# First channel layer in units of 512 columns, narrower mask products and new list priorities in a fused block-sparse attention and mixer kernel

## The chip, the cores and the metric

The kernel runs on one core of one Trainium2 chip. The metric is the device time in microseconds; of several runs the median counts. TensorE (PE in the profile) does the matrix products, VectorE (DVE) and ScalarE (ACT) the element-wise work, GpSimd (POOL) some of the mask and most of the load issues, SyncE (SP) the other transfers.

## The reference

Block-sparse attention for 4 batches of 8 heads, 768 positions, 64 columns per head, and then a token and channel mixer on its output, reshaped to 4 x 768 x 512.

```python
scores = scale * np.matmul(q, k.transpose(0, 1, 3, 2))
mask = np.abs(blk_i - blk_j) <= window              # blocks of 32, window 1
mask = mask | (blk_i == 0) | (blk_j == 0) | (blk_i == n_blocks - 1) | (blk_j == n_blocks - 1)
for qb in range(n_blocks):
    for kb in sampled_blocks[qb]:
        mask[qb * block:(qb + 1) * block, kb * block:(kb + 1) * block] = True
scores = np.where(mask, scores, -1000000000.0)
...                                                  # softmax over the keys
x = attn @ v
h = np.maximum(xt @ w_tok1, 0.0) @ w_tok2            # token layers, 768 -> 256 -> 768
u = x + h.transpose(0, 2, 1)
h2 = np.maximum(u @ w_ch1, 0.0) @ w_ch2              # channel layers, 512 -> 1536 -> 512
out = u + h2
```

## The kernel before

Heads are worked in 16 pairs p, four pairs to a batch. Position s of the sequence sits on partition s // 6, in chunk s % 6, so that each of six chunks holds 128 positions that lie six apart. For each pair, k and q are transposed (on TensorE for pairs 1 to 7, L711, with copies by VectorE or ScalarE; by transposing transfers on SP's queue from pair 8 on, L671). The queries of a pair go in three parts t of 256, the keys in three parts jj of 256. A group of four score matmuls (L770, two key chunks by two heads) fills two of the eight PSUM banks; ScalarE takes the exponential of it in one instruction (L783) and frees the banks. The value products (L895, 24 matmuls of 65 columns per (p, t), the last column a sum) go to one bank, and VectorE normalises them (L909, L910) into the tile x of the batch.

For pairs 0 to 4 the mask is part of the scores: 24 more rows of k and q (88 rows in all) add a large negative number. From pair 5 on (`NT0`), the scores of the two heads are matmuls of 64 rows each, the three groups of a (p, t) are issued together as a unit of twelve, and the mask is multiplied into the exponentials `et` by VectorE, 3072 elements per partition in one instruction (L800).

When the four pairs of a batch are through, the two token layers follow (L976 and L998; for batch 0 in narrower pieces per pair, L1030 and L1052), with a relu between them and an addition (L1006, L1061), then the turn of u to uT (by transposing transfers, L955, for batch 0 by TensorE, L1074), and the channel layers in `ch(b)`: the first (L1110) takes 12 x 2 units of four matmuls of 384 columns, each unit with a relu by ScalarE (L939) or VectorE (L941) into `rc`; the second (L1138) takes 12 matmuls of 512 columns for each of six chunks, and VectorE adds u (L1150) and SP sends the rows out.

The order on every engine is set while the program is built, by the class `Planner`. It keeps a clock, one free time per engine and a list of operations with priorities; at each step it gives a free engine the ready operation of the lowest priority number, with costs in ns that are written beside each operation. TensorE's work comes in streams with priorities of their own: scores 0, value products 1, token layers `toks` (batch 0: `tokp`), transposes `trp`, channel layers 4. Operations of VectorE and ScalarE have the priorities `relu`, `norm`, `add`, `cut` (mask products), `fin` (last additions), `relayk` and `relayv` (copies of k, q and v), `ev2` and `ev4` (copies of transposed k and q). `later`, `unseen` and the `h_` values decide whether a bank of the scores may be lent to another product; `grace` says by how much a relu on ScalarE may delay an exponential; `m2` delays the readiness of a transpose.

Of the kernel before, what the change touches and what calls it, by code (L numbers as in the profile page):

```python
# [8 lines left out]
FP32 = mybir.dt.float32  # L9
# [4 lines left out]
KN = dict(  # L14
    tokp=2.5, trp=2.6, toks=1.2, later=1400.0, unseen=1500.0, h_pm=1200.0, h_po=1800.0,
    h_ch1=1400.0, h_ch2=3500.0, relayk=0.8, relayv=4.6, fin=2.1, relu=0.85, cut=5.0, norm=0.6,
    add=3.0, ev2=2.0, ev4=3.3, grace=400.0, m1=0.0, m2=150.0, nt0=5, cuts=2, xbar=8,
)
# [37 lines left out]
class Planner:  # L56
# [13 lines left out]
    def __init__(self, slots):  # L70
        self.now = 0.0
        self.free_at = {"pe": 0.0, "act": 0.0, "dve": 0.0, "sp": 0.0}
        self.streams = []
        self.ops = []
        self.count = 0
        self.slots = {tag: [Ev(0.0)] * n for tag, n in slots.items()}
        self.banks = [Ev(0.0)] * 8
        self.shared = 0
        self.lend = None
        self.exp_pending = 0  # L80
# [73 lines left out]
    def step(self):  # L154
# [29 lines left out]
        else:  # L184
            nxt.append(self.free_at["pe"])
        for eng in ("act", "dve", "sp"):
            if self.free_at[eng] > self.now:
# [42 lines left out]
def kernel(  # L230
# [12 lines left out]
    nc = tc.nc  # L243
# [9 lines left out]
    NET = 3  # L253
    NPE = KN["xbar"]
    NT0 = KN["nt0"]
    TOKP = KN["tokp"]
# [380 lines left out]
    def relayout(p):  # L637
        lays = {}
        for nm in ("k", "q", "v") if p >= NT0 else ("v",):
            raw = raws.pop((nm, p))  # L640
# [38 lines left out]
    def transposes(p):  # L679
        yield lambda: ("v", p) in raws  # L680
        if p >= NPE:
# [77 lines left out]
    et_rel = {u: Ev() for u in units}  # L759
    VISIT = 3  # L760
    CUTS = (((0,), (1,), (2,)), ((0, 1), (2,)), ((0, 1, 2),), ((0,), (1, 2)))[KN["cuts"]]

    def scores(s, bank, done, rel, exps):
# [30 lines left out]
        for group in CUTS:  # L794
            if group[-1] != jj:
                continue

            def cut(eng, lo=group[0], n=len(group)):
                et = ets[p, t][:, lo : lo + n, :, :, :].rearrange("k j i h q -> k (j i) h q")
                nc.vector.tensor_tensor(  # L800
                    out=et, in0=et,
                    in1=free(mask[:, 2 * lo, 256 * t : 256 * t + 256], 0,
                             [[S, 2 * n], [0, 2], [1, 256]]),
                    op=ALU.mult,
                )

            ev = P.op(("dve",), {"dve": 158.0 + 537.0 * len(group)},
                      [exps[x] for x in group] + [mask_there], cut, prio=KN["cut"])
            for x in group:
                alias(et_there[p, t, x], ev)  # L810

    def qk_deps(p, t, jj):
# [24 lines left out]
    def qk_stream():  # L837
        exps = {}
        while queue:
# [5 lines left out]
            if p < NT0:  # L845
# [13 lines left out]
                continue  # L859

            evs = [(Ev(), Ev()) for _ in range(3)]

# [12 lines left out]
            if t == 2:  # L875
                alias(qk_done[p], evs[2][0])

# [55 lines left out]

    def relu_op(o, i, deps, prio):
        n = i.free_size()

        def emit(eng):
            if eng == "act":
                nc.scalar.activation(out=o(), in_=i, func=AF.Relu)  # L939
            else:  # L940
                nc.vector.tensor_scalar(  # L941
                    out=o(), in0=i, scalar1=0.0, scalar2=None, op0=ALU.max
                )

        return P.op(("dve", "act"), {"dve": dve_psum(n), "act": act_cost(n)}, deps, emit, prio=prio)
# [19 lines left out]
    def tok(b, g):  # L965
# [21 lines left out]
        a_t = sbw.tile([128, 2, 256], BF16, tag="a_t", name=f"a_t{b}_{g}")  # L987
        a_there = relu_op(lambda: a_t[:, :, :], box["pm"][:, :, :], [last], urgent)
        alias(rel, a_there)
# [29 lines left out]
    def tok_first(p):  # L1019
# [21 lines left out]
        a_t = sbw.tile([128, 2, 256], BF16, tag="a_t", name=f"a_t0_{p}")  # L1041
        a_there = relu_op(lambda: a_t[:, :, 0:128], box["pm"][:, :, :], [last], urgent)
        alias(rel, a_there)
# [50 lines left out]
    def ch(b):  # L1094
# [3 lines left out]
        box = {}  # L1098
        for cc in range(12):
            for sh in range(2):  # L1100
                last, rel, pbox = Ev(), Ev(), {}
                for dmc in range(4):
                    first = dmc == 0
                    def emit(cc=cc, sh=sh, dmc=dmc, rel=rel, pbox=pbox):
                        if dmc == 0:
                            pbox["pm"] = take_bank("ch1", rel, [512], FP32)
                            if cc == 0 and sh == 0:
                                P.take("rc", rc_rel)
                                box["rc"] = sbw.tile([128, 12, S], BF16, tag="rc", bufs=2, name=f"rc{b}")
                        nc.tensor.matmul(  # L1110
                            out=pbox["pm"][:, 0:384], lhsT=w_ch1[:, dmc, 128 * cc : 128 * cc + 128],
                            rhs=st[b]["uT"][:, dmc // 2, 3 * sh : 3 * sh + 3, dmc % 2, :],
                            start=(dmc == 0), stop=(dmc == 3),
                        )
                    tags = [("ch1", 1)] if first else []
                    if first and cc == 0 and sh == 0:
                        tags.append(("rc", 1))
                    deps = [st[b]["uT_there"][dmc], ch1_there[dmc]]
                    if b == 0 and first:
                        deps.append(turned)  # L1120
                    yield 162.5, deps, tags, emit, last if dmc == 3 else None
                ev = relu_op(
                    lambda cc=cc, sh=sh: box["rc"][:, cc, 384 * sh : 384 * sh + 384],
                    pbox["pm"][:, 0:384], [last], KN["relu"],
                )
                alias(rel, ev)
                rc_there[cc, sh] = ev
        alias(st[b]["uT_rel"], last)
# [3 lines left out]
        for sc, lo, n in parts:  # L1132
            last, rel, pbox = Ev(), Ev(), {}
            for cc in range(12):
                def emit(sc=sc, cc=cc, lo=lo, n=n, rel=rel, pbox=pbox):
                    if cc == 0:
                        pbox["pm"] = take_bank("ch2", rel, [DM], FP32)
                    nc.tensor.matmul(  # L1138
                        out=pbox["pm"][:, 0:n], lhsT=box["rc"][:, cc, 128 * sc : 128 * sc + 128],
                        rhs=w_ch2[:, cc, lo : lo + n], start=(cc == 0), stop=(cc == 11),  # L1140
                    )
                yield n / 2.4 + 2.5, [rc_there[cc, sc // 3], ch2_there[cc // 3]], [("ch2", 1)] if cc == 0 else [], emit, last if cc == 11 else None

# [56 lines left out]
    P.stream(KN["toks"], tok_stream((1, 2, 3)))  # L1200
    P.stream(4, ch_stream())
    P.stream(1.8, mask_stream())
# [22 lines left out]
    def pull():  # L1225
        while loads:
# [5 lines left out]
            else:  # L1232
# [6 lines left out]
                t, home = min(free_from)  # L1239
                load_pair(x, t, home)  # L1240
                tenant[home] = x
                if x == NP - 1:
                    all_loaded.t = arrive["v", x].t
            loads.popleft()
# [36 lines left out]
```

## Time and profile before

| | us |
|---|---|
| median of 4 runs (250.08 to 253.68) | 250.79 |
| the profiled execution | 251.17 |
| its span | 249.4 |
| TensorE busy | 242.8 (97%) |
| VectorE busy | 170.9 (69%) |
| ScalarE busy | 170.2 (68%) |
| GpSimd busy | 49.7 (20%) |

The busy time of a matmul is modelled and includes time in which it is in the pipeline, so that a mean of 326 ns stands for matmuls that start 162 ns apart. The page divides the span into 40 slices of 6.2 us and gives the busy share of each engine as a digit. The chain is followed back from the last instruction, at each step to what released it. In the tables of groups, the columns after the bar are busy time and mean duration, and after the second bar the idle time before the group and what ended it.

### The profile page before, as it was taken

Reading aid. Unit: us, or ns where it says so; the run is one execution under the profiler, and the core shown is the slowest. Engines: PE = TensorE matmul, PEld = TensorE weight load, DVE = VectorE, ACT = ScalarE, POOL = GpSimd, SP = SyncE. Lnnn points to the kernel's source line nnn. Section 1 sums busy time; section 2 is a strip of 40 time slices with the busy share of each in tenths; the row PEclk is TensorE's granted clock in tenths of the full one; section 3 lists DMA queues with packets and bytes.
Section 4 is the critical chain, followed back from the end, with each engine's and each line's share of the span. In section 5 each row is a group of like instructions: output and inputs, shape, how many; then the busy total and the mean of one; then the engine's idle time right before and its main releaser. Section 6 shows DMA issues by size and latency. Waiting matters only on the chain.

```text
span 249.4 us, 6594 instructions
## 1 busy us (share of the span) xinstructions
PE 242.8 (97%) x2807; PEld 162.8 (65%) x2807; DVE 170.9 (69%) x321; ACT 170.2 (68%) x210; POOL 49.7 (20%) x86
## 2 busy tenths in 40 slices
PE   8799999999999999999999999999999999999994
PEld 3488999976676566666856556566766565555444
DVE  5884677779897799977867687979869745200222
ACT  5799999988957977489577877648768800377000
POOL 8845989667500000000000000000000000000000
PEclk9999999999999999999999999999999999999999
DMA  7999999999976861843033171330030024300132
GB/s 166 165 216 203 213 202 204 206 200 201 201 116 127 108 172 42 126 120 75 3 63 66 39 100 53 85 108 3 3 63 3 3 84 101 132 3 0 42 120 93
DMA packets 42461, 26.35 MB, mean 106 GB/s; under 512 B 23680, under 2 KB 38800, under 8 KB 42432
## 3 DMA queue, kind: packets, MB, share of 16 engines
q0 software_dynamic: 15104, 12.98, 33.1%
q1 hardware_dynamic: 26784, 12.56, 21.5%
q8 instruction: 22, 0.36, 0.6%
q10 hardware_dynamic: 544, 0.39, 0.5%
q14 instruction: 7, 0.06, 0.1%
HBM read 26.74 MB, written 6.29 MB: 132 GB/s over the span
## 4 chain that ended last, share of the span: by engine, by line
PE 91%; DMA 2%; ACT 2%; POOL 2%; DVE 1%; issue 1%; POOLq 0%; DVEq 0%
PE banks L1110 26%; PE banks L1138 25%; PE banks L770 16%; PE banks L895 14%; PE banks L976 3%; PE banks L998 3%; DMA qraw<-in_q_dram 2%; ACT et L783 2%; PE banks L711 2%; PE banks L1052 1%; PE banks L1030 1%; DVE et L800 1%; PE banks L1074 1%; POOL ktb L401 0%; POOL ktb L405 0%
## 5 line engine op out<-in xcount | busy, mean ns | idle before, releaser
L783 ACT ACTIVATE et<-banks 128x1024 bf16<-128x1024 f32 x144 | 137.2, 1025 | 27.9 <-PE banks L770 27.6
L1110 PE MATMUL banks<-uT,w_ch 128*128 128x384 bf16 x384 | 68.4, 326 | 0.0
L1138 PE MATMUL banks<-w_ch,rc 128*128 128x512 bf16 (+2 forms) x312 | 67.7, 363 | 0.0
L800 DVE TENSOR_TENSOR et<-et,mask 128x3072 bf16<-128x3072 bf16 x33 | 57.8, 1753 | 1.7 <-ACT et L783 1.5
L770 PE MATMUL banks<-qtb,ktb 64*128 64x256 bf16 (+1 forms) x576 | 54.4, 271 | 0.5 <-ACT et L783 0.3
L1110 PEld LDWEIGHTS <-w_ch 128*128 128x128 bf16 x384 | 35.6, 98 | 23.6 <-issue 2.7
L895 PEld LDWEIGHTS <-et 128*128 128x128 bf16 x1152 | 43.6, 97 | 6.6 <-issue 1.1
L895 PE MATMUL banks<-vaug,et 128*128 128x65 bf16 x1152 | 46.7, 193 | 0.1
L1138 PEld LDWEIGHTS <-rc 128*128 128x128 bf16 x312 | 28.0, 98 | 28.2 <-issue 2.1
L939 ACT ACTIVATE rc<-banks 128x384 bf16<-128x384 f32 x55 | 26.8, 492 | 22.1 <-PE banks L1110 21.6
L770 PEld LDWEIGHTS <-ktb 64*128 64x128 bf16 (+1 forms) x576 | 31.9, 95 | 15.2 <-issue 12.2
L1150 DVE TENSOR_TENSOR o<-banks,x 128x512 f32<-128x512 f32 x23 | 15.8, 688 | 31.0 <-PE banks L1138 30.8
L909 DVE RECIPROCAL recip<-banks 128x4 f32<-128x4 f32 x48 | 8.7, 182 | 26.5 <-PE banks L895 26.3
L941 DVE TENSOR_SCALAR rc<-banks 128x384 bf16<-128x384 f32 x41 | 22.3, 554 | 5.3 <-PE banks L1110 4.3
L910 DVE TENSOR_TENSOR x<-banks,recip 128x256 bf16<-128x256 f32 x48 | 20.4, 425 | 1.7
L1006 DVE TENSOR_TENSOR x<-banks,x 128x512 bf16<-128x512 f32 x18 | 11.5, 681 | 3.1 <-PE banks L998 3.1
L976 PE MATMUL banks<-x,w_tok 128*128 128x256 bf16 x72 | 9.5, 273 | 0.0
L998 PE MATMUL banks<-a_t,w_tok 128*128 128x256 bf16 x72 | 9.3, 274 | 0.0
L998 PEld LDWEIGHTS <-w_tok 128*128 128x128 bf16 x72 | 7.7, 126 | 0.7 <-issue 0.4
L976 PEld LDWEIGHTS <-w_tok 128*128 128x128 bf16 x72 | 6.6, 98 | 2.2 <-issue 0.8
L331 POOL DMA_DIRECT2D vraw<-in_v_dram x10 | 7.4, 737 | 2.7 <-DVE recip L909 1.0
L615 POOL COPY mask<-maskb 128x240 bf16<-128x240 bf16 (+1 forms) x18 | 7.5, 481 | 0.0
(94 smaller groups left out, 131.2 us busy)
## 6 DMA issues: line engine op xcount, KB each, us to landing
out_dram<-o SPq DMA_DIRECT2D x23, 256.0 KB, 2.0
w_ch<-in_moe_w_ch_dram POOLq DMA_DIRECT2D x8, 384.0 KB, 9.8
vraw<-in_v_dram POOLq DMA_DIRECT2D x10, 192.0 KB, 7.9
kraw<-in_k_dram POOLq DMA_DIRECT2D x9, 192.0 KB, 7.6
qraw<-in_q_dram POOLq DMA_DIRECT2D x9, 192.0 KB, 7.9
w_tok<-in_moe_w_tok_dram POOLq DMA_DIRECT2D x2, 384.0 KB, 10.4
qf<-in_v_dram POOLq DMA_DIRECT2D x4, 192.0 KB, 7.4
klay_first<-in_k_dram POOLq DMA_DIRECT2D x2, 192.0 KB, 7.9
```

The lines of the kernel that those rows point to most:

```text
L770: nc.tensor.matmul(out=ps[:, hd, 256 * i : 256 * i + 256], lhsT=ktb[n][rows, h, 256 * jj + 128 * i : 256 * jj + 128 * i + 128], rhs=qtb[n] ...
L783: nc.scalar.activation(out=ets[p, t][:, jj, :, :, :].rearrange("k i h q -> k h i q"), in_=ps.rearrange("k h (i q) -> k h i q", i=2), func= ...
L800: nc.vector.tensor_tensor(out=et, in0=et, in1=free(mask[:, 2 * lo, 256 * t : 256 * t + 256], 0, [[S, 2 * n], [0, 2], [1, 256]]), op=ALU.mult,)
L895: nc.tensor.matmul(out=po[:, hd, c, :], lhsT=et[:, jj, i, hd, 128 * c : 128 * c + 128], rhs=va[:, hd, 2 * jj + i, 0:65], start=(jj == 0 an ...
L910: nc.vector.tensor_tensor(out=free(xs[b][:, pb // 2, 2 * t, 128 * (pb % 2) : 128 * (pb % 2) + 128], 0, [[64, 2], [256, 2], [1, 64]],), in0 ...
L939: nc.scalar.activation(out=o(), in_=i, func=AF.Relu)
L941: nc.vector.tensor_scalar(out=o(), in0=i, scalar1=0.0, scalar2=None, op0=ALU.max)
L976: nc.tensor.matmul(out=box["pm"][:, t, :], lhsT=w_tok1[:, sc, 128 * t : 128 * t + 128], rhs=xs[b][:, g, sc, :], start=(t == 0 and sc == 0) ...
L998: nc.tensor.matmul(out=ubox["pm"][:, i, :], lhsT=w_tok2[:, t, :, 2 * s2 + i], rhs=a_t[:, t, :], start=(i == 0 and t == 0), stop=(i == 1 an ...
L1110: nc.tensor.matmul(out=pbox["pm"][:, 0:384], lhsT=w_ch1[:, dmc, 128 * cc : 128 * cc + 128], rhs=st[b]["uT"][:, dmc // 2, 3 * sh : 3 * sh + ...
L1138: nc.tensor.matmul(out=pbox["pm"][:, 0:n], lhsT=box["rc"][:, cc, 128 * sc : 128 * sc + 128], rhs=w_ch2[:, cc, lo : lo + n], start=(cc == 0 ...
L1150: nc.vector.tensor_tensor(out=o[:, :].rearrange("p (g e) -> p g e", g=2), in0=pbox["pm"][:, :].rearrange("p (g e) -> p g e", g=2), in1=st[ ...
```

## The change

It has three parts. The first channel layer takes units of 512 columns: for each of the 12 column blocks `cc` of the weights one unit of four matmuls of 512 columns (chunks 0 to 3), and for each two blocks one unit of eight matmuls of 256 columns (chunks 4 and 5 of both). The mask product leaves out the first 4 and last 4 queries of each part of 256 (`EDGE`), which lie in the first or the last block and see all keys. The priorities and margins of the planner get other values. Other new names in the diff (`vd`, `tri`, `spb`, `kq`, the engine "pool" of the planner) have values with which they change no instruction.

```diff
-    tokp=2.5, trp=2.6, toks=1.2, later=1400.0, unseen=1500.0, h_pm=1200.0, h_po=1800.0,
-    h_ch1=1400.0, h_ch2=3500.0, relayk=0.8, relayv=4.6, fin=2.1, relu=0.85, cut=5.0, norm=0.6,
-    add=3.0, ev2=2.0, ev4=3.3, grace=400.0, m1=0.0, m2=150.0, nt0=5, cuts=2, xbar=8,
+    tokp=1.7, trp=2.0, toks=-0.5, later=1000.0, unseen=800.0, h_pm=800.0, h_po=1800.0,
+    h_ch1=1100.0, h_ch2=2500.0, relayk=3.5, relayv=4.6, fin=4.1, relu=0.85, cut=3.2, norm=2.3,
+    add=2.4, ev2=0.9, ev4=2.0, grace=0.0, m1=0.0, m2=450.0, nt0=5, cuts=2, xbar=8, chs=4.0,
+    c512=1, vd=16, kq=0, tri=0, edge=4, spb=0, relayv2=3.0,
...
     def transposes(p):
-        yield lambda: ("v", p) in raws
+        yield lambda: ("v" if p == 0 else "q", p) in raws
...
             def cut(eng, lo=group[0], n=len(group)):
-                et = ets[p, t][:, lo : lo + n, :, :, :].rearrange("k j i h q -> k (j i) h q")
+                w = 256 - 2 * EDGE
+                et = free(ets[p, t][:, lo, 0, 0, EDGE : EDGE + 1], 0, [[512, 2 * n], [256, 2], [1, w]])
                 nc.vector.tensor_tensor(
                     out=et, in0=et,
-                    in1=free(mask[:, 2 * lo, 256 * t : 256 * t + 256], 0,
-                             [[S, 2 * n], [0, 2], [1, 256]]),
+                    in1=free(mask[:, 2 * lo, 256 * t + EDGE : 256 * t + EDGE + 1], 0,
+                             [[S, 2 * n], [0, 2], [1, w]]),
                     op=ALU.mult,
                 )
 
-            ev = P.op(("dve",), {"dve": 158.0 + 537.0 * len(group)},
+            ev = P.op(("dve",), {"dve": 158.0 + (537.0 - 4.2 * EDGE) * len(group)},
...
-        for cc in range(12):
-            for sh in range(2):
-                last, rel, pbox = Ev(), Ev(), {}
-                for dmc in range(4):
...
-                            out=pbox["pm"][:, 0:384], lhsT=w_ch1[:, dmc, 128 * cc : 128 * cc + 128],
-                            rhs=st[b]["uT"][:, dmc // 2, 3 * sh : 3 * sh + 3, dmc % 2, :],
-                            start=(dmc == 0), stop=(dmc == 3),
...
+        if KN["c512"]:
+            units = []
+            for cc in range(12):
+                units.append([(cc, 0, 4, 0)])
+                if cc % 2:
+                    units.append([(cc - 1, 4, 2, 0), (cc, 4, 2, 256)])
+        else:
+            units = [[(cc, 3 * sh, 3, 0)] for cc in range(12) for sh in range(2)]
+        for u in units:
+            last, rel, pbox = Ev(), Ev(), {}
+            for x in range(4 * len(u)):
+                cc, lo, n, at = u[x // 4]
+                dmc = x % 4
...
+                        out=pbox["pm"][:, at : at + 128 * n], lhsT=w_ch1[:, dmc, 128 * cc : 128 * cc + 128],
+                        rhs=st[b]["uT"][:, dmc // 2, lo : lo + n, dmc % 2, :],
+                        start=(x == 0), stop=(x == 4 * len(u) - 1),
...
+            ev = relu_op(
+                lambda cc=cc, lo=lo, m=m, k=len(u): box["rc"][:, cc : cc + k, 128 * lo : 128 * lo + m],
+                lambda pbox=pbox, m=m, k=len(u): pbox["pm"][:, 0 : m * k].rearrange("p (a b) -> p a b", a=k),
+                [last], KN["relu"], m * len(u),
+            )
...
-                yield n / 2.4 + 2.5, [rc_there[cc, sc // 3], ch2_there[cc // 3]], [("ch2", 1)] if cc == 0 else [], emit, last if cc == 11 else None
+                yield n / 2.4 + 2.5, [rc_there[cc, sc], ch2_there[cc // 3]], [("ch2", 1)] if cc == 0 else [], emit, last if cc == 11 else None
...
-    P.stream(4, ch_stream())
+    P.stream(KN["chs"], ch_stream())
```

## The prediction

> **What bounds the kernel now.** I read the slices and the chain on the page first, then the chain in order of time, the timelines of TensorE and ScalarE over the first 52 us, and the groups by shape.
>
> ```profile
> PE   8799999999999999999999999999999999999994
> ACT  5799999988957977489577877648768800377000
> PE 91%; DMA 2%; ACT 2%; POOL 2%; DVE 1%; issue 1%; POOLq 0%; DVEq 0%
> ```
>
> TensorE is busy in every slice and carries 91% of the chain. A busy TensorE can still be one that waits, so I compared the chain in order of time with what the matmuls need:
>
> ```profile
> 215.03 15.60 PE banks L1110 x96
> 230.63 15.61 PE banks L1138 x96
> ```
>
> 96 matmuls of 384 columns take 15.60 us, 162.5 ns each. In the same way the chain gives 215.5 ns for 512 columns ("x4", 0.86 us), 109 ns for 256 columns (12 in 1.31 us on L976), 56 ns for 128 columns, 0.44 us for a group of four scores of pairs 0 to 4, 0.86 us for a unit of twelve scores of later pairs (0.76 us, and 0.1 us before it), 0.73 us for 24 value products. With these I priced the whole program order of TensorE and set the sum beside the starts in the timeline. Between 19 and 52 us nothing is left over, in the last 42 us 0.03 us, between 52 and 208 us under 0.7 us. Nearly all of TensorE's lost time is in the first 19 us:
>
> ```profile
> 9.75 0.60 PE L770 MATMUL banks<-qtb,ktb 88*128 88x256 bf16 x4
> 10.19 0.33 PE L711 MATMUL banks<-ident,kraw 128*128 128x128 bf16 x3
> 11.32 0.51 PE L711 MATMUL banks<-ident,qraw 128*128 128x128 bf16 x6 [0.80 <-DMA qraw<-in_q_dram]
> 11.66 0.60 PE L770 MATMUL banks<-qtb,ktb 88*128 88x256 bf16 x4
> ...
> 18.66 0.22 PE L1030 MATMUL banks<-x,w_tok 128*128 128x128 bf16 x1
> 19.14 0.60 PE L770 MATMUL banks<-qtb,ktb 88*128 88x256 bf16 x4 [0.26 <-ACT et L783]
> ```
>
> The transposes of pair 1's q stand in the order before the fifth group of scores and wait for a load; start to start, 0.96 us are lost between 10.19 + 0.17 and 11.32. ScalarE shows what this costs:
>
> ```profile
> 8.68 2.85 ACT L783 ACTIVATE et<-banks 128x1024 bf16<-128x1024 f32 x3 [0.19 <-PE banks L770]
> 12.30 33.42 ACT L783 ACTIVATE et<-banks 128x1024 bf16<-128x1024 f32 x35 [0.77 <-PE banks L770]
> 45.62 0.38 ACT L939 ACTIVATE a_t<-banks 128x256 bf16<-128x256 f32 x1
> ```
>
> From 12.30 us ScalarE runs 35 exponentials without a gap, 33.42 / 35 = 0.955 us each. TensorE is held to this pace until about 20 us (the 0.43 us lost before 19.14, 0.24 us before the group at 18.23), and after that both are full. So the 0.77 us that ScalarE idles at 11.5 us is carried to the end.
>
> ```profile
> L1110 PE MATMUL banks<-uT,w_ch 128*128 128x384 bf16 x384 | 68.4, 326 | 0.0
> L800 DVE TENSOR_TENSOR et<-et,mask 128x3072 bf16<-128x3072 bf16 x33 | 57.8, 1753 | 1.7 <-ACT et L783 1.5
> L939 ACT ACTIVATE rc<-banks 128x384 bf16<-128x384 f32 x55 | 26.8, 492 | 22.1 <-PE banks L1110 21.6
> L941 DVE TENSOR_SCALAR rc<-banks 128x384 bf16<-128x384 f32 x41 | 22.3, 554 | 5.3 <-PE banks L1110 4.3
> ```
>
> VectorE and ScalarE stand idle waiting for TensorE, not the reverse.
>
> **What the Trainium skill says.** "TensorE: Matmul & The Clock Gate", section "Wait — 56ns, not 53.3ns?": warm matmuls start N / 2.4 GHz plus about 2.5 ns apart. The trace agrees: 162.5, 215.5, 109 and 56 ns. Its section "Step-by-step: what each phase is for" has matmuls stay in program order while weight loads may be pulled ahead; the trace agrees, the wait for q at 11.32 us holds scores that need nothing of it. "VectorE: DVE Perf Modes", section "Mode 2×_1P — pack two bf16 into one 32-bit read": two results a cycle need 16-bit types, step 1 and 4-byte alignment. The mask product's 3072 elements in 1753 ns are 1.75 per ns, so it has that mode.
>
> **The change part by part.**
>
> Units of 512 columns. Per batch 96 matmuls of 384 columns (15.60 us) become 48 of 512 and 48 of 256: 48 x 215.5 + 48 x 109 = 15.58 us. TensorE gets nothing. The weight loads stay 96 and are hidden under 256 columns already (L976). The relus fall from 96 to 72. By the two orders ScalarE has 38 instead of 55, VectorE 34 instead of 41. With the rows for 512 columns of the token layer (597 ns on ScalarE, 687 ns on VectorE): before 55 x 0.492 + 41 x 0.554 = 49.8 us, after 38 x 0.597 + 34 x 0.687 = 46.0 us. These 3.8 us lie beside TensorE; nothing in the chain waits for a relu of this layer, so I count them as 0. In the last batch all 18 relus are on ScalarE, 0.6 us each against 0.86 us of matmuls per unit, so they still hide. At the turn to the second layer, its first rows no longer need the very last unit; there was no stall there (230.63 follows 215.03 + 15.60), so nothing is gained.
>
> Mask products. 12 x 8 = 96 of 3072 elements go: 96 / 1.92 = 50 ns each by the mode above, 33 x 0.05 = 1.7 us of VectorE, beside TensorE. The offset of 4 elements is 8 bytes, so the mode should stay; that rows are now broken does not matter by the copies into vaug (768 elements in rows of 64, 349 ns from qf). I take 1.70 us each; the bounds are 1.65 and, if the mode is lost, 2976 / 0.96 + 150 = 3.25 us.
>
> The order. Multiplied out, the work of TensorE is the same in both orders within 0.1 us, and there are 33 units of twelve scores in each, so the 0.1 to 0.2 us around each of these stays too. POOL's queue has the same order; SP's has the same 57 transfers, a few of them exchanged (the turn of batch 1's second half now ahead of pair 12's). The turn that matters, batch 3's, was issued at 209.04 us and needed at 214.9; the order after gives it 40 instead of 37 second-layer matmuls (8.6 us instead of 8.0) and its three additions are no longer parted. So only waits can go or come:
>
> - Start. The fourth group of scores stays at 9.75 us (it waits for the second exponential). Then six k transposes, to 10.5. The fifth group waits for the third exponential's banks, about 10.6, and starts at 10.7 instead of 11.66. The fifth exponential then starts when the fourth ends, 11.53 instead of 12.30: 0.77 us. The q transposes now come after the seventh group, at about 13.2; q has landed at 11.3. Their copies on VectorE end near 14.9 (15.1 before), and pair 1's first scores start at about 15.7 instead of 16.39. The one k transpose of pair 2 that moves to 13.5 finds its data landed (issued 6.80, 6.4 us to landing: 13.2). The twelfth exponential ends at 11.53 + 8 x 0.955 = 19.2, so the 14th group starts at 19.3 instead of 20.12. From there the order has 29.8 us to the last score of pair 4 (29.9 before). Sum: -0.8 to -1.0 us; I take -0.9. If a wait on VectorE (its copies for pairs 1 and 2 changed places with the normalisations) eats it, the end is 0.
> - Middle. Before, the largest stall is 0.27 us at 156.8 us, where value products wait for a mask product that stood behind a relu. It goes, since the two token layers now run whole. In its place the second token layer starts 0.9 to 1.4 us after the first; it needs 0.2 us plus 0.60 or 0.69 us for the relu. For batch 1's first half the next scores come 3.0 us after the last ones, and the exponentials need 2.7: 0.1 us. From the end of a unit's scores to its value products the order leaves 4.6 to 7.2 us; needed are 2.68 (exponentials), 0.03 and 1.70, so 4.5 with the signal. I take 0 for the middle, bounds -0.6 and +0.8.
> - End: same matmuls and same last transfers, 0.
>
> The profiled execution took 251.17 us (span 249.4); less 0.9 it is 250.3. It stands 0.38 above the median of the four, 250.79, so the forecast for a median is 249.9.
>
> **The rivals.** (a) Nothing is gained: the start gains 0.8 us but new short waits of 0.05 to 0.2 us in the middle give it back, as many units have only 0.1 us to spare: 250.8 us. For it: before, gaps were filled just as tightly; against: the shorter mask product adds 0.05 us to each. (b) All waits go: 0.96 + 0.3 (before 9.75) + 0.9 (13 to 20 us) + 0.6 in the middle = 2.8, less the 0.6 that ScalarE's pace forbids: -2.2, 248.6 us. Against it: groups 13 and 14 stay bound by the exponentials. (c) Slower: the mask product does not keep its pace in broken rows. Its place is between the last exponential and the value products; it decides from about 1.85 us on. At 2.1 us the 16 units with at most 4.85 us of room each wait 0.2 to 0.3 us: +4 us, 253.9 us after the gain; with the mode lost VectorE alone gets 33 x 1.5 = 50 us more, which exceeds its idle time between 52 and 204 us. The copies in rows of 64 speak against it. (d) The change does not do what it says on TensorE, its 256-column matmuls waiting for weights: 12 in 1.31 us exclude more than 1 us.
>
> **How the numbers follow.** Forecast (-0.4 to -1.4 us) 0.54; (a) 0.22; (b) 0.14, of which 0.08 reaches 1%; (c), (d) or a stall that I have not seen 0.10. One per cent, 2.5 us, is about what a measurement of this kernel can tell from no change. Faster by more needs 248.3 or less: 0.08 of (b) and 0.04 for idle time that my prices hide, 0.12. Slower by more needs 253.3: 0.10. The rest, 0.78, is within. The range takes in the forecast, (a) and most of (b), and leaves out (c): 248.4 to 251.5.
>
> **What would show it.** Right: the fifth exponential at about 11.5 us without a gap before it, the mask product at 1.70 us, the start of the first channel layer 0.8 to 1 us earlier, TensorE's busy total lower by no more than 1 us, ScalarE and VectorE each some 2 us less busy. Wrong: value products that wait for mask products in many units, token layers that wait for their relu, or a span more than 2 us away from 248.5.

## The result and the profile after

| | us |
|---|---|
| before, median of 56 runs (249.83 to 254.1) | 250.38 |
| after, median of 35 runs (249.28 to 251.1) | 249.79 |
| ratio, with its 95% interval | 0.9977 (0.9968 to 0.9986) |
| the profiled execution of after | 249.9 |
| its span | 248.2 |

The ratios leave out runs that took more than 1.5% longer than the fastest of their kernel, and are estimated over all that are left, so that they need not be the quotients of the medians.

The change gains 0.58 us by the ratio, 0.59 between the medians. In the profiles the span falls by 1.2 us (249.4 to 248.2), twice as much; where the other half comes from is the main question of the experiments.

The page of after, slices, chain and groups, in the order in which those of before were shown:

```profile
PE   7899999999999999999999999999999999999994
...
ACT  5899999988867776588567876588778600266000
...
PE 95%; DMA 2%; ACT 1%; DVE 1%; SPq 0%; issue 0%; ACTq 0%
...
L1197 PE MATMUL banks<-uT,w_ch 128*128 128x512 bf16 (+1 forms) x384 | 68.6, 326 | 0.0
...
L812 DVE TENSOR_TENSOR et<-et,mask 128x2976 bf16<-128x2976 bf16 x33 | 56.2, 1704 | 1.7 <-ACT et L794 0.9
...
L1017 ACT ACTIVATE rc<-banks 128x512 bf16<-128x512 f32 x38 | 22.7, 597 | 21.7 <-PE banks L1197 21.1
...
L1019 DVE TENSOR_SCALAR rc<-banks 128x512 bf16<-128x512 f32 x34 | 23.2, 688 | 6.3 <-PE banks L1197 6.0
```

TensorE's share of the chain rises from 91% to 95%. These 4%, some 10 us, are not waiting that has gone, for the span fell by 1.2 us; the chain takes another way. That of before comes over GpSimd and the load of pair 1's q and reaches TensorE at 11.32 us, and between 14.3 and 19.1 us it runs over exponentials; that of after comes over a load of pair 0's q and a cast of it by ScalarE and reaches TensorE near 7.3 us. The first channel layer costs TensorE the same as before (68.6 against 68.4 us of modelled busy time); the mask product is at 1704 ns; the relus are down to 22.7 + 23.2 = 45.9 us from 49.1 (26.8 + 22.3), all of it on ScalarE.

The start and the end of after, from the timelines of TensorE, ScalarE and VectorE (start, duration, then the instruction and how many in a row; the bracket is idle time before it):

```profile
9.53 0.60 PE L781 MATMUL banks<-qtb,ktb 88*128 88x256 bf16 x4 [0.41 <-DVE qtb L479]
9.97 0.50 PE L722 MATMUL banks<-ident,kraw 128*128 128x128 bf16 x6
10.45 0.60 PE L781 MATMUL banks<-qtb,ktb 88*128 88x256 bf16 x4
...
12.88 0.50 PE L722 MATMUL banks<-ident,qraw 128*128 128x128 bf16 x6
...
8.46 5.73 ACT L794 ACTIVATE et<-banks 128x1024 bf16<-128x1024 f32 x6 [0.19 <-PE banks L781]
...
50.67 0.59 PE L1197 MATMUL banks<-uT,w_ch 128*128 128x512 bf16 x2
...
245.07 0.29 DVE L1250 TENSOR_TENSOR o<-banks,x 128x128 f32<-128x128 f32 x1 [0.38 <-PE banks L1231]
```

In before the first channel matmul and the last addition are these:

```profile
51.54 0.65 PE L1110 MATMUL banks<-uT,w_ch 128*128 128x384 bf16 x3
...
246.26 0.29 DVE L1157 TENSOR_TENSOR o<-banks,x 128x128 f32<-128x128 f32 x1 [0.38 <-PE banks L1138]
```

The fifth group of scores starts at 10.45 us instead of 11.66, the q transposes come at 12.88 without a wait, and ScalarE runs six exponentials from 8.46 us without a gap, the fifth at 11.18 instead of 12.30. The first channel matmul starts at 50.67 us instead of 51.54. So 0.87 us of the difference lie ahead of it, and from there to the end of the span it is 248.2 - 50.67 = 197.53 us against 249.4 - 51.54 = 197.86: another 0.33.

Not all of the 0.87 us is the work of the new order. The fourth group of scores, which comes ahead of the wait for pair 1's q, starts at 9.53 us instead of 9.75. The first four groups need pair 0's q, which ScalarE casts as soon as its load is there, first in before and then in after:

```profile
6.82 0.62 ACT L461 CAST qlay_first<-qf 128x512 bf16<-128x512 f32 x1 [1.21 <-DMA qf<-in_q_dram]
...
6.60 0.62 ACT L463 CAST qlay_first<-qf 128x512 bf16<-128x512 f32 x1 [0.91 <-DMA qf<-in_q_dram]
```

The two kernels issue this load at the same time (1.79 and 1.78 us), and it landed 0.22 us earlier in the execution of after. From the fourth group to the first channel matmul before takes 51.54 - 9.75 = 41.79 us and after 50.67 - 9.53 = 41.14, so 0.65 us are left for the order and the wait.

### The profile page after: what moved, and what is told of

Read it like the earlier page. It is cut to its first block, busy times and chain, and to the rows that moved or that the text cites. A ratio compares the mean times of both kernels' runs of the same rounds, so it can differ in the third digit from the quotient of the medians.

```text
span 248.2 us, 6578 instructions
## 1 busy us (share of the span) xinstructions
PE 242.4 (98%) x2807; PEld 162.7 (66%) x2807; DVE 170.8 (69%) x314; ACT 166.8 (67%) x193; POOL 49.4 (20%) x86
## 3 DMA queue, kind: packets, MB, share of 16 engines
q1 hardware_dynamic: 26784, 12.56, 22.7%
## 4 chain that ended last, share of the span: by engine, by line
PE 95%; DMA 2%; ACT 1%; DVE 1%; SPq 0%; issue 0%; ACTq 0%
PE banks L1231 26%; PE banks L1197 26%; PE banks L781 18%; PE banks L974 14%; PE banks L1054 3%; PE banks L1076 3%; PE banks L722 2%; DMA qf<-in_q_dram 2%; PE banks L1130 1%; PE banks L1108 1%; PE banks L1152 1%; ACT et L794 0%; ACT qlay_first L463 0%; DVE qtb L479 0%; PE banks L471 0%
## 5 line engine op out<-in xcount | busy, mean ns | idle before, releaser
L1197 PE MATMUL banks<-uT,w_ch 128*128 128x512 bf16 (+1 forms) x384 | 68.6, 326 | 0.0
L1231 PE MATMUL banks<-w_ch,rc 128*128 128x512 bf16 (+2 forms) x312 | 68.6, 363 | 0.0
L812 DVE TENSOR_TENSOR et<-et,mask 128x2976 bf16<-128x2976 bf16 x33 | 56.2, 1704 | 1.7 <-ACT et L794 0.9
L974 PEld LDWEIGHTS <-et 128*128 128x128 bf16 x1152 | 44.2, 97 | 7.7 <-issue 0.8
L1231 PEld LDWEIGHTS <-rc 128*128 128x128 bf16 x312 | 27.1, 97 | 27.6 <-issue 3.4
L1017 ACT ACTIVATE rc<-banks 128x512 bf16<-128x512 f32 x38 | 22.7, 597 | 21.7 <-PE banks L1197 21.1
L1019 DVE TENSOR_SCALAR rc<-banks 128x512 bf16<-128x512 f32 x34 | 23.2, 688 | 6.3 <-PE banks L1197 6.0
L988 DVE RECIPROCAL recip<-banks 128x4 f32<-128x4 f32 x48 | 8.7, 182 | 23.2 <-PE banks L974 22.2
L1054 PE MATMUL banks<-x,w_tok 128*128 128x256 bf16 x72 | 8.8, 273 | 0.0
L1076 PEld LDWEIGHTS <-w_tok 128*128 128x128 bf16 x72 | 7.9, 125 | 0.9 <-issue 0.2
L1054 PEld LDWEIGHTS <-w_tok 128*128 128x128 bf16 x72 | 7.0, 98 | 1.9
```

The lines of the kernel that those rows point to most:

```text
L812: nc.vector.tensor_tensor(out=et, in0=et, in1=free(mask[:, 2 * lo, 256 * t + EDGE : 256 * t + EDGE + 1], 0, [[S, 2 * n], [0, 2], [1, w]]), ...
L974: nc.tensor.matmul(out=po[:, hd, c, :], lhsT=et[:, jj, i, hd, 128 * c : 128 * c + 128], rhs=va[:, hd, 2 * jj + i, 0:65], start=(jj == 0 an ...
L1017: nc.scalar.activation(out=o(), in_=i(), func=AF.Relu)
L1019: nc.vector.tensor_scalar(out=o(), in0=i(), scalar1=0.0, scalar2=None, op0=ALU.max)
L1054: nc.tensor.matmul(out=box["pm"][:, t, :], lhsT=w_tok1[:, sc, 128 * t : 128 * t + 128], rhs=xs[b][:, g, sc, :], start=(t == 0 and sc == 0) ...
L1076: nc.tensor.matmul(out=ubox["pm"][:, i, :], lhsT=w_tok2[:, t, :, 2 * s2 + i], rhs=a_t[:, t, :], start=(i == 0 and t == 0), stop=(i == 1 an ...
```

## Experiments: the wait for q, and the units alone

Ratios are to before, which ran on the same chip in each group, with 95% intervals. The kernels are written in the changed code, which with the old values and `c512=0, edge=0` is before.

**Pair 1's q loaded earlier** (`q_load_early`): before, with all priorities and TensorE's order kept; GpSimd issues the load ahead of its work for the second half of the block indices.

```diff
-    ind_part(2, 4)
-    load_pair(1, 5.2 * US, 1, ("q", "v"))
+    load_pair(1, 5.2 * US, 1, ("q",))
+    ind_part(2, 4)
+    load_pair(1, 5.2 * US, 1, ("v",))
```

> The kernel before with TensorE's order unchanged; only the load of pair 1's q is issued ahead of GpSimd's second mask-index step instead of behind it, 1.3 us earlier. Theory (the gain is the wait for q at the start): the six transposes no longer wait, the fifth exponential starts near 11.6 us instead of 12.30, and the kernel is 0.4 to 0.8 us faster than before. Rivals (the gain comes from the units of 512 columns, or from the narrower mask products): no change, within 0.2 us.

Measured: 249.94 us, ratio 0.9985 (0.9974 to 0.9996), some 0.4 us faster by the ratio and 0.2 between the medians (250.15 for before). Its profile has no wait for q, and its 13 runs spread from 249.64 to 250.41 where the 19 runs of before beside it reach from 249.83 to 251.26. The wait is worth something, but less than the 0.8 us that the profile of before showed, and what goes is above all the upper end of the spread.

**The transposes of q held back, or put forward, by the planner** (`q_moved` is before with the first line, `q_back` the changed kernel with the second):

```diff
-                deps = [there_at]
+                deps = [there_at] if (nm, p) != ("q", 1) else [there_at, Ev(12e3)]
+                deps = [there_at] if (nm, p) != ("q", 1) else [Ev(there_at.t - 200.0)]
```

> The kernel before with one more condition for the transposes of pair 1's q, a planned time of 12 us, so that the planner puts them behind the sixth and seventh group of scores; the list after that follows from it. Old priorities, units of 384 columns, full mask products. Theory: the fifth group of scores starts near 10.7 us, the kernel is 0.4 to 0.9 us faster, unless the planner's later list brings waits of its own. Rivals: within 0.2 us of before.

> The changed kernel, in which the planner takes pair 1's q to land 0.2 us earlier and so puts four of its six transposes ahead of the fifth group of scores again; from pair 6 on the list is the changed one. Theory: the wait at the start comes back and most of the gain is lost, 0 to 0.3 us faster than before. Rivals: it keeps the gain of 0.6 us, since units of 512 columns and narrower mask products are still in it.

Measured: `q_moved` 263.86 us, ratio 1.053 (1.0497 to 1.0563); `q_back` 252.16 us, ratio 1.0086 (1.0066 to 1.0107). `q_back` is outside what either theory gave; for `q_moved` the expectation had allowed for it, with a later list that has waits of its own. `q_back` has the wait, 2.0 us long: the order has the transposes ready some 0.5 us earlier than before, and q landed at 11.99 us instead of 11.32. But it is some 2 us slower than before, not faster, and its profile, of an execution of 253.49 us, has 1.0 us of further waits after 50 us, for normalisations and a mask product. So it does not give the price of the wait. `q_moved` tells nothing of the wait either: a different dependency of one transpose changed the planner's whole later list, and that list waits 3.6 us for the turned sums uT and 3.5 us for mask products. These are sizes from its profiled execution, which at 269.0 us was the longest of the seven, and they do not account for the median.

**Units of 512 columns alone** (`c512_old`), with all old priorities and the full mask product:

```diff
-    c512=0, edge=0
+    c512=1, edge=0
```

> The kernel before with units of 512 columns alone: old priorities, full mask products. The relus cost some 3.8 us less of ScalarE and VectorE together. Theory: TensorE's order has the same work and the same start, so within 0.3 us of before. Rival (the units bring the gain): 0.6 us faster.

Measured: 268.76 us, ratio 1.0741 (1.0718 to 1.0764). That was not foreseen. The waits of TensorE (in total, times, longest), three places in its timeline, and the windows about the first of them (busy time of the engines, then the granted clock):

```profile
PE banks L1198 <- DMA uT<-x: 11.6, 3, 5.0
...
110.95 2.72 PE L1198 MATMUL banks<-uT,w_ch 128*128 128x512 bf16 x6 [4.98 <-DMA uT<-x]
...
174.29 2.72 PE L1198 MATMUL banks<-uT,w_ch 128*128 128x512 bf16 x6 [4.57 <-DMA uT<-x]
...
230.90 11.37 PE L1198 MATMUL banks<-uT,w_ch 128*128 128x512 bf16 x58 [2.06 <-DMA uT<-x]
...
108.00:112.00 4.00, 1.04 (x3) 0.40 (x3) 0.00 (x0) 0.00 (x0) 0.00 (x0) 0.60 0.51 98
112.00:114.00 2.00, 2.00 (x8) 0.58 (x8) 0.00 (x0) 0.89 (x2) 0.00 (x0) 0.50 0.00 0
114.00:116.00 2.00, 2.00 (x18) 1.26 (x14) 0.00 (x0) 1.99 (x3) 0.00 (x0) 0.60 0.00 0
116.00:118.00 2.00, 2.00 (x13) 1.02 (x12) 1.40 (x3) 1.17 (x2) 0.00 (x0) 1.00 0.67 131
```

At the start of the first channel layer of batches 1, 2 and 3 TensorE has run out of other work and waits for the second half of uT, which is turned by a transfer on SP's queue after the last addition of the token layers. After each such wait the clock stands at 0.50 for some microseconds, and matmuls of 512 columns start 0.44 us apart (six in the 2.65 us from 110.95 on) instead of 0.22. The waits (11.6 us) and some 5 us of clock make up most of the 18.6 us.

To compare lists I priced TensorE's order as in the prediction and took the work that it puts between the last matmul of a batch's token layers and the first channel matmul on the second half of uT. In `c512_old` the sum came 7.6 us after that matmul (103.36 to 110.95), so I expected that less room than that would be waited out:

| kernel | room, batches 1, 2, 3 (us) |
|---|---|
| before | 8.5, 8.5, 8.3 |
| after | 10.9, 10.7, 9.1 |
| `c512_old` | 2.5, 2.9, 2.8 |
| `q_moved` | 1.9, 7.4, 3.1 |
| `order_only` (below) | 4.6, 7.2, 7.2 |
| `c512_toks` (below) | 11.2, 14.9, 10.6 |

## Experiments: one part of the list at a time

To change an order in one place and nowhere else on TensorE, the next two kernels take TensorE's stream picks from a written list, that of before or of after, with six picks moved; priorities decide on the other engines as they did.

**The q transposes behind the seventh group, in before's list** (`head_moved`), **and ahead of the fifth, in after's list** (`after_head_back`). In the picks, 0 is a group of scores, 1 a piece of value products, 3 one transpose, 8 the mask's matmuls:

```diff
 before's list
-... 0 3x9 0 1x2 0 1 8 0 3x6 1 ...
+... 0 3x3 0 1x2 0 1 8 0 3x12 1 ...
 after's list
-... 0 3x6 0 1x3 0 8 0 3x7 1 ...
+... 0 3x12 0 1x3 0 8 0 3 1 ...
```

> TensorE has the order of before, except that the six transposes of pair 1's q stand behind the seventh group of scores instead of ahead of the fifth; units of 384 columns and the full mask product are kept. Theory H (the gain of the change is the wait for q at the start): the fifth exponential starts at about 11.5 us instead of 12.3, and the time falls by 0.6 to 0.9 us, to 249.3 to 249.7 with before at 250.2. Rival M (the gain lies in the middle, in shorter mask products and fewer relus): no change, within 0.2 us of before.

> The changed kernel with TensorE's order kept, except that the six transposes of pair 1's q stand ahead of the fifth group of scores, as in before. Theory H: the wait for q is back, the time rises by 0.6 to 0.9 us over the changed kernel and comes to that of before, ratio 1.000 to 1.002. Rival M: the time stays that of the changed kernel, ratio about 0.9977.

Measured: `head_moved` 250.77 us, ratio 1.0036 (1.0024 to 1.0048); `after_head_back` 250.67 us, ratio 1.0018 (1.0008 to 1.0029), 0.9 us above after. The second has the time that theory H gave, but only in part by the wait: in its profile 1.20 us more than in after pass from the fourth group of scores to the first channel matmul (42.34 against 41.14), of which 0.50 are the wait for q, and ScalarE idles another 0.50 us ahead of the eighth exponential. The first contradicts the theory: the same move makes the old list slower. ScalarE's timeline in `head_moved` shows where:

```profile
8.07 5.64 ACT L810 ACTIVATE et<-banks 128x1024 bf16<-128x1024 f32 x6 [0.37 <-PE banks L797]
14.31 10.29 ACT L810 ACTIVATE et<-banks 128x1024 bf16<-128x1024 f32 x11 [0.60 <-PE banks L797]
25.14 20.13 ACT L810 ACTIVATE et<-banks 128x1024 bf16<-128x1024 f32 x21 [0.53 <-PE banks L797]
```

There is no gap ahead of the fifth exponential, but twelve transposes in one lump now stand before the eighth group (0.60 us), and at 24.2 us value products wait 0.38 us for a normalisation on VectorE. After's list parts that lump: six transposes of q and one of pair 2's k, then eight value products, then the eighth group, and the other k transposes later.

**The new priorities with the old units and the full mask product** (`order_only`), **and the units with one new priority** (`c512_toks`):

```diff
 order_only, against after
-    c512=1, edge=4
+    c512=0, edge=0
 c512_toks, against before
-    toks=1.2, c512=0
+    toks=-0.5, c512=1
```

> The changed kernel's priorities with units of 384 columns and the full mask product: its start is that of the changed kernel, and the order parts from it where the first channel layer begins. Priced, its order leaves 4.6, 7.2 and 7.2 us of TensorE's work between the last matmul of a batch's token layers and the first channel matmul that needs their turned sum (before: 8.5, 8.5, 8.3; changed: 10.9, 10.7, 9.1; the units alone with the old priorities: 2.5, 2.9, 2.8, where the turned sum came 7.6 us after that matmul). Theory U (a list is slow where this room falls under some 7.6 us): a stall of about 3 us at batch 1's first channel layer and up to 0.4 us at the other two, with a lower TensorE clock after it: 252.5 to 255 us. Rival V (large losses come only with the units of 512 columns under old priorities): the new priorities alone give the gain of the start, 249.5 to 249.9.

> Before with units of 512 columns, and of the priorities only that of the token layers set to the new value (-0.5 instead of 1.2); the start is that of before, the mask product is full. Priced room ahead of the three turned sums: 11.2, 14.9 and 10.6 us. Theory U: none of the stalls of the units alone (11.6 us in three waits) comes back, and the time is that of before within 0.5 us, since units of 512 give TensorE nothing. Rival V (the units themselves hurt unless all priorities fit): 255 us or more.

Measured: `order_only` 252.96 us, ratio 1.0114 (1.0101 to 1.0127); `c512_toks` 253.21 us, ratio 1.0097 (1.0083 to 1.0112). The waits of TensorE from 50 us on, of the first and then of the second:

```profile
PE banks L975 <- DVE et L813: 1.0, 1, 1.0
...
PE banks L782 <- ACT et L795: 0.3, 1, 0.3
...
PE banks L975 <- DVE et L813: 0.8, 1, 0.8
PE banks L1055 <- DVE x L990: 0.5, 1, 0.5
```

`order_only` has the time that theory U gave, but not by the wait that it named: near 107 us, where channel work runs out, the list sets scores and value products one behind the other, and these wait for exponentials and a mask product. In `c512_toks` the waits for uT are gone, as theory U had it, and all but 3 of the 18.6 us with them; but it stays 1% above before with waits of other kinds, so neither theory foresaw it. The room ahead of uT explains the large losses and not the last per cent. Units of 384 columns with the new priorities lose, and so do units of 512 with the old ones or with this single new one: the values fit the units, and no part of the gain can be assigned to either alone.

## Experiments: a second profile of before, and the mask product

**Before once more** (`before_again`), unchanged:

> The kernel before once more, unchanged, for a second profiled execution. Theory R (when pair 1's q lands differs from execution to execution; of nine profiles, those of the units alone and of the units with one new priority have before's order at the start and no wait for q): the wait for q is below 0.4 us or absent, the span is some 0.5 to 1 us shorter than 249.4, and the stretch from the first channel matmul to the end takes 197.85 us again. Theory F (the wait belongs to the order): 0.8 us are waited for q again and the fifth exponential starts 4.8 us after the first.

Measured: 249.81 us in its one run, span 248.1. Its cast of pair 0's q by ScalarE, and its timeline of TensorE:

```profile
5.80 0.62 ACT L461 CAST qlay_first<-qf 128x512 bf16<-128x512 f32 x1 [0.18 <-DMA qf<-in_q_dram]
...
9.15 0.60 PE L770 MATMUL banks<-qtb,ktb 88*128 88x256 bf16 x4 [0.16 <-ACT et L783]
...
9.96 0.51 PE L711 MATMUL banks<-ident,qraw 128*128 128x128 bf16 x6
...
50.25 0.65 PE L1110 MATMUL banks<-uT,w_ch 128*128 128x384 bf16 x3
```

Theory R holds for the wait and for the last stretch. The same program in the same order has q at 9.96 us here and waited for it until 11.32 in the first profile. The fifth exponential starts at 10.94 us, 4.26 after the first, and the first channel matmul at 50.25, earlier even than in after. From there to the end it is 248.1 - 50.25 = 197.85 us, as in the first profile. `c512_old` and `c512_toks` have the same start and load and do not wait for q either (in `c512_toks` the whole start is late, its fourth group at 10.82 us), so that it is waited for in one of four profiles.

The span is 1.3 us shorter, more than the 0.5 to 1 us that theory R gave, because two loads came earlier. Pair 0's q let its cast start at 5.80 us instead of 6.82, and the fourth group of scores stands at 9.15 instead of 9.75: 0.60 us. From there to the first channel matmul it is 41.10 us, against 41.79 with the wait for pair 1's q: 0.69. After has 41.14, so in these profiles its start is no shorter than that of before without the wait.

That last stretch hardly varies: 197.85, 197.86, 197.85 and 197.92 us in the four profiles with before's list (before, `before_again`, `q_load_early`, `head_moved`), and 197.52 to 197.54 in the five with after's from there on (after, `after_head_back` and the three below). Up to the start of VectorE's last addition, which the timelines give to 0.01 us, it is 194.72 to 194.80 us in the four and 194.40 or 194.41 in the five. These 0.32 us are the part of the gain that every one of the nine profiled executions shows.

**The full mask product in the changed kernel** (`edge0`) **and three columns instead of four left out at each edge** (`edge3`), the orders of all engines kept (the planner still reckons with the cost of the product with four left out):

```diff
-    edge=4
+    edge=0        # edge0
+    edge=3        # edge3
```

> The changed kernel with the mask product back at its full width (3072 elements instead of 2976) and the order of every engine kept. Theory P (the mask product is hidden): it takes 1.75 instead of 1.70 us, VectorE is 1.7 us busier, the time stays that of the changed kernel, ratio to before 0.997 to 0.9985, and the stretch from the first channel matmul to the end stays at 197.5 us. Rival E (the 0.3 us that the changed kernel gains in that stretch come from the shorter mask products): 197.85 us there, ratio about 0.999.

> The changed kernel, order kept, with three columns left out at each edge instead of four: 3000 elements in rows of 250 that begin 6 bytes into each block instead of 8. If the two results a cycle need a start on 4 bytes, nothing is lost in time and the product falls out of its mode only where a row starts off such a boundary: 6 bytes is off it, so 3000 / 0.96 = 3.1 us each, VectorE 46 us busier, nearly every unit late for its value products: 260 to 280 us. Rival: the boundary doesn't matter, 1.71 us each and the time of the changed kernel, 249.8.

Measured: `edge0` 249.56 us, ratio 0.9974 (0.9958 to 0.9989); `edge3` 249.89 us, ratio 0.9981 (0.997 to 0.9993). Both are within the interval of after. The mask products of `edge3`:

```profile
L813 DVE TENSOR_TENSOR et<-et,mask 128x3000 bf16<-128x3000 bf16 x33 | 57.1, 1732 | 1.7 <-ACT et L795 0.9
```

The stretch from the first channel matmul to the end takes 197.54 and 197.52 us. So the narrower product gives VectorE 1.6 us (57.8 to 56.2) and the kernel nothing that these runs can tell, and rows that begin 6 bytes into a block run at 3000 / 1732 = 1.73 results per ns, like whole rows (3072 / 1753 = 1.75).

**The start of before, without its wait, ahead of after's middle** (`hybrid`), an attempt at a better kernel:

```diff
-    norm=2.3, m2=450.0
+    norm=0.6, m2=150.0
-    ind_part(2, 4)
-    load_pair(1, 5.2 * US, 1, ("q", "v"))
+    load_pair(1, 5.2 * US, 1, ("q",))
+    ind_part(2, 4)
+    load_pair(1, 5.2 * US, 1, ("v",))
```

> The changed kernel with the start of before: the transposes of pairs 1 and 2 are not held back (150 ns instead of 450), normalisations come first on VectorE (0.6 instead of 2.3), and pair 1's q is loaded ahead of the indices' second part; from batch 1's first channel layer on, TensorE's order is that of the changed kernel. Theory R: without the wait for q the start of before is the shorter one, so this beats both, 249.3 to 249.7 us, 0.1 to 0.5 below the changed kernel. Theory F and rival H (the gain lies in the moved transposes): no better than the changed kernel, 249.8 to 250.3.

Measured: 249.79 us, ratio 0.9975 (0.9955 to 0.9995), the same as after, and so just short of the 249.3 to 249.7 of theory R. Its profile has 41.11 us from the fourth group to the first channel matmul, after has 41.14: once q is not waited for, the two starts are not told apart. No version found beats after by more than the noise.

## Why the prediction came out right, step by step

The forecast was 249.9 us and 249.79 was measured, but that they agree to 0.1 us is luck. The median of before, of four runs, was taken 0.41 us too high (250.79; 250.38 in 56 runs), the start was credited with 0.64 us too much, and 0.32 us in the middle were not counted; the three make up for each other. The gain was forecast as 0.9 us and is 0.58.

- **What bounds the kernel.** Held. TensorE's prices held in after too: batch 3's first channel layer again takes 15.60 us for 96 matmuls.
- **Units of 512 columns, counted as 0.** Right for TensorE's work: priced over all batches the order is 0.1 us shorter from the first channel matmul on. The relus came to 45.9 us (46.0 predicted; before they were 49.1, where the prediction has 49.8) and stay hidden. What the step left out is that the units need a list of their own; the order after provided one, so the total did not suffer, but `c512_old` shows that the 0 is no property of the units.
- **Mask product, -50 ns each and nothing in time.** Right: 1704 ns instead of 1753, and `edge0` has the time of after. The reason given, a start on 4 bytes, was not needed, as `edge3` shows.
- **Start, -0.9 us.** It looks right in the two profiled executions (0.87 at the first channel matmul), but 0.22 of that lie ahead of the fourth group of scores, which the prediction had at 9.75 us in both, and come from an earlier landing of pair 0's q. It is wrong as a term for the median. This is the mis-sized term. It took the wait for q, 0.80 us by the profile, as part of the order. It is a matter of when a load lands in an execution: absent in `before_again`, and worth 0.2 (medians) to 0.4 us (ratio) by `q_load_early`. What the start gives to the median is what remains of the gain, 0.58 - 0.32 = 0.26 us. The forecast set the profiled execution 0.38 us above the median of four runs; above the median of 56 it stood 0.79, which was the sign of an unusual execution. That `head_moved` is slower shows besides that a moved step gains only with the places of its neighbours.
- **Middle, 0 with bounds of -0.6 and +0.8.** It is -0.32. By starts less prices, the losses from the first channel matmul on fall from 4.24 to 4.02 us, and the priced work by 0.10. (These losses include the 0.1 us ahead of each of the 33 units of twelve scores, which the prediction put into their price; without it before has 0.9 us, where the prediction says under 0.7.) The stall near 156 us, 0.27 us of value products, went as the step said, and it was in `before_again` and `head_moved` too; two smaller ones, ahead of second token matmuls (0.11) and of value products (0.09), went with it. New ones are 0.17 us more within second token layers, and 0.12 within the channel layers. The first is one wait of 0.25 us ahead of the fifth matmul of a second token layer, at 73.10 us. It is not for the relu, on which the step had looked: that ended at 72.33. The chain of after has an exponential there, from 72.03 to 73.06 us, so by the chain the product waited for the bank that this one frees. The step let the new stalls cancel the old one; they took back about 0.3 of 0.5 us.
- **End, 0.** Right: 96 matmuls of 512 columns and the last additions and transfers as before.
- **Rivals.** (a), nothing gained, was the nearest: new short waits gave part back, but not all. (b) failed on the start: the wait that was to go is absent in three of the four profiles with before's start. (c) and (d) did not occur: 1.73 results per ns even from 6 bytes on, and 15.60 us for the layer. The stall "not seen" did not occur in after; of the partial versions, `c512_old`, `order_only` and `c512_toks` ran into stalls that no theory had named.
- **The signs.** The fifth exponential, the mask product, the first channel layer and TensorE's total came as said. ScalarE is 3.4 us less busy (170.2 to 166.8), but VectorE is not (170.9 to 170.8). The prediction's own rows have its relus grow, 41 x 0.554 to 34 x 0.687 us, and that takes back part of what the mask products give.

What remains open: from the profiles alone the 0.26 us at the start are not shown to be there in each execution. Between the fastest runs, 249.83 and 249.28 us, after is 0.55 ahead, where only 0.32 come from the middle. No profile shows after in so fast an execution, and its own start varies too: with the same list, `edge0` and `edge3` take 41.40 and 41.20 us from the fourth group to the first channel matmul. Nor was it settled which of the new priorities removes the stall near 156 us.

## What to carry to other kernels

A wait for a load near the start can be a property of one execution: before a gain is sized by it, hold the profiled execution against the spread of the runs, and profile the same kernel a second time. The duration of a later stretch, here from the first channel matmul to the end, repeats to less than 0.1 us and shows a gain that totals blur. Where a planner makes the order, its priorities and the sizes of its units are one setting: try them together, and look first at how much work a list leaves ahead of each long transfer that TensorE depends on.

## What the runs showed of the hardware

- Waits of 2.06 us (`c512_old`) and 2.39 us (`q_moved`, ahead of 231.43 us) were followed by half of TensorE's clock; one of 2.02 us near 11 us of `q_back` was not, its clock stayed at 1.00. In `c512_old` 2.06 us of idle time ahead of 230.90 us are followed by this (windows of 2 us, the clock is the third number from the end):

```profile
230.00:232.00 2.00, 1.10 (x5) 0.52 (x5) 0.00 (x0) 0.47 (x1) 0.00 (x0) 0.91 0.50 160
232.00:234.00 2.00, 2.00 (x10) 1.08 (x9) 0.00 (x0) 0.72 (x2) 0.00 (x0) 0.50 0.00 0
234.00:236.00 2.00, 2.00 (x9) 1.00 (x8) 0.00 (x0) 0.79 (x2) 0.00 (x0) 0.73 0.00 0
```

  That is (0.09 + 0.50 + 0.27) x 2 = 1.7 us lost, about as much again as the wait. The clock fell only when the matmuls ran again: in windows of 1 us it is 1.00 from 230 to 231 us and 0.82 from 231 to 232. The Trainium skill, "TensorE: Matmul & The Clock Gate", section "What's actually happening", gives a halved clock after about 3.4 us of idle time; that it halves and comes back agrees, the idle time that it took was shorter in these two places.
- The mask product keeps its pace from a start at 6 bytes, 1.73 results per ns against 1.75 in whole rows. "Vector Engine (DVE) Microarchitecture Reference", section "5.1 Performance modes — why throughput varies by op and dtype", says that alignment to 4 bytes makes no difference; the 1732 ns agree with it, and not with the condition that the prediction took from "VectorE: DVE Perf Modes".
- The arrival of one and the same load differed by at least 1.3 us between two executions of before (pair 1's q, issued at 5.4 us: 11.3 us, and 9.96 or earlier), that of pair 0's q, issued at 1.8 us, by 1.0 us (6.8 and 5.8).
